# Moving key copies and scalings between VectorE, ScalarE and POOL in the first chunk of a block-sparse attention with an MLP behind it

## The chip, the cores and the metric

The kernel runs on one core of a Trainium2 chip. The metric is the device time of one execution in microseconds (us); lower is better. A core has a matmul engine (TensorE, PE in the profile), VectorE (DVE), ScalarE (ACT), GpSimd (POOL) and a queue that issues DMAs (SyncE, SP). Each engine works through its own queue in order and waits for the others by semaphores.

## The reference

```python
def _attn_ref(q, k, v, sampled_blocks):          # q, k, v: (4, 8, 768, 64)
    scores = scale * np.matmul(q, k.transpose(0, 1, 3, 2))
    # blocks of 32: kept are |i - j| <= 1, the first and last block of
    # rows and of columns, and three sampled blocks per row of blocks
...
    scores = np.where(mask, scores, -1000000000.0)
    attn = np.exp(scores - np.max(scores, axis=-1, keepdims=True))
    attn = attn / (np.sum(attn, axis=-1, keepdims=True) + 1e-09)
    return np.matmul(attn, v)

def _moe_ref(x, w_in, w_out):                    # (3072, 512), (512, 2048), (2048, 512)
    h = np.maximum(x @ w_in, 0.0)
    return h * h @ w_out
```

The attention's output, 3072 tokens of 8 heads x 64, is the input of the second part. The mask is never built: each block of 32 rows gathers eight blocks of keys (first, last, three sampled, three neighbours).

## The kernel before, in words

**Tiles and chunks.** The 3072 tokens are 24 tiles of 128 (four batches of six). The text calls them k0 to k23. A chunk is three tiles. A tile's attention is done in two halves of four heads: k0u0, k0u1, k1u0 and so on (class `Half`, L380). The first and the last block of rows of a batch see all keys; they are done for two heads at a time by class `Whole` (L581), four per batch, W0 to W3 here.

**A half's steps.** `scores` (L427) multiplies queries with gathered keys on TensorE; `maxima` (L444) reduces on VectorE and scales the negative maximum (L453); `exps` (L491) runs four exponentials on ScalarE with that maximum as bias; `turn` (L503) transposes on TensorE; `copies` (L513) takes the transposes out of PSUM on ScalarE; `values` (L524) multiplies with gathered values; `norm` (L540) divides and transposes on VectorE; `high` (L865) casts the result to the matmul's 32-bit format (xh) on POOL, for the very last half on ScalarE; `low` (L869) subtracts it on VectorE to get the rest (xl). `Whole` has the same steps; its `copies` (L676) have two parts (512 and 256 columns), the first on ScalarE, the second on VectorE (L683).

**Keys.** For tiles k0 to k5 the gathered keys (tile `KG`) are copied on chip from a whole batch of keys in SBUF (`kn`). `copy_keys` (L275) is a generator: per half it copies the two static blocks (L338), the neighbouring blocks (L308, or a wide copy of `key_windows`, L303, and two edges, L315), then three sampled blocks for each block of rows (L290), and it yields after each block of rows. Eight such steps make a tile. The generators of k3, k4 and k5 stand in the list `later`, to which `loads` (L553) appends them as the chunk goes on.

**Weights.** A weight block of 128x512 comes by a POOL DMA as 64-bit numbers (`craw`, L785). `cut` (L787) makes 32-bit numbers of it with two ScalarE operations (L801, L803) and `cut_bits` (L806) with two VectorE operations (L812, L813). `cut_next` (L829) issues one round of these stages, each for a different block. `split` (L842) makes a cast (wi, on ScalarE in the first chunk) and a difference (POOL, L848) for the matmuls. Buffers of `craw` and of these split weights rotate through seven.

**The order of work.** Every queue's order is written out by the program. Until the first dense matmul a loop counts steps (`now`, L1044): units W0 to W3, k0u0, ..., k2u1 begin five steps apart, each resumes after the lags of `LAG_0`; at step 8 `prepare` (L1026) issues the rest of the copies for k0 to k2 and five weight loads; from `FIXED_0` on one of the copies in `fixed` (L1038) is issued per step on ScalarE: static values (L212) and the value windows of k2 (L224, L228); at the steps of `CUT_0` a `cut_next`; from step 44 on, at every second step, one step of k3's keys.

**The dense stretch.** Then `moe(0)` (L959) runs the two matmuls of the first chunk: `hidden` (L883) and `project` (L926), 16 blocks each. It yields some six times per block, and at each yield (L1071 to L1081) a step of the first generator in `later` is issued, every third time a `cut_next`, and the second chunk's attention is advanced (halves 12 steps apart from step 0 on, `LAG_1`). Chunks 1 to 7 follow in the same way.

Of the kernel before, what the change touches and what calls it, by code (L numbers as in the profile page):

```python
# [15 lines left out]
ALU = mybir.AluOpType  # L16
# [12 lines left out]
NJ = P // BLK  # L29
# [5 lines left out]
SCALE = 0.125  # L35
# [12 lines left out]
UC = 3  # L48
# [19 lines left out]
G_AT = 6  # L68

STEP_0 = 5  # L70
STEP_1, FIRST_1 = 12, 0
LAG_1 = {**LAG, "v": 10, "x": 3, "t": 6, "v0": 5, "n": 0}
LAG_0 = {"s": 2, "x": 2, "t": 3, "c": 2, "v0": 2, "n": 2, "r": 1, "l": 3, "l0": 8}
SPLIT_0 = 52

CUT_0 = (30, 5)
CUT_1 = 3

KEYS_0, KEYS_1 = 8, 44


FIXED_0 = 7
KEYS_N = 2
MOVED = 6


# [10 lines left out]
def tile_block_sparse_attention_moe(ctx: ExitStack, tc, kd, knd, qd, qgd, vd, vnd, samp, const, wcat, out):  # L97
# [9 lines left out]
    nc = tc.nc  # L107
# [134 lines left out]
    def groups(t):  # L242

        return tuple(range(1 if t == 0 else 0, NJ - 1 if t == NT - 1 else NJ))
# [51 lines left out]
    def key_windows(k, u, copy):  # L296

        b, t = order[k]
        kg, kn = st["kg", b, t][:, :, :, 2 * u : 2 * u + 2], st["kn", b, u]
        if 0 < k < UC:  # L300
            dst = kg[:, :, NJ:NK].rearrange("p j a i c -> p j a (i c)")
            src = kn[:, NJ * t : NJ * t + NJ].rearrange("p a i c -> p a (i c)").unsqueeze(1)
            copy(dst, src.broadcast_to(list(dst.shape)))  # L303
            return
        js = groups(t)
        c = NJ * t + js[0] - 1
        for n in range(3):
            copy(kg[:, js[0] : js[-1] + 1, NJ + place(k, 0, n)], kn[:, c + n : c + n + len(js)])  # L308
# [8 lines left out]
    later = []  # L317
# [62 lines left out]
    class Half:  # L380
# [63 lines left out]
        def maxima(self):  # L444
            m = self.m = rot.tile([P, 2, 2], F32, tag="m", name=f"m{self.name}", bufs=4)
            at = self.rows
            for e in range(2):
                nc.vector.tensor_reduce(  # L448
                    m[at, e], self.sb[e][at].rearrange("p (i c) -> p i c", i=2), axis=AX, op=ALU.max
                )  # L450
            self.p = rot.tile([P, 4, 2, NJ, BLK], F32, tag="p", name=f"p{self.name}", bufs=PBUFS)
            if not self.moved:
                nc.vector.tensor_scalar(m[at], m[at], -SCALE, None, op0=ALU.mult)  # L453
                return
            for e in range(2):
                nc.vector.tensor_tensor(  # L456
                    self.p[at, 2 * e : 2 * e + 2].rearrange("p h c a s -> p h (c a s)"),
                    self.sb[e][at].rearrange("p (i c) -> p i c", i=2),
                    m[at, e].unsqueeze(2).broadcast_to([at.stop, 2, NSLOT]),
                    op=ALU.subtract,  # L460
                )
# [28 lines left out]

        def exps(self):  # L491
            at = self.rows
            for e in range(2):
                for i in range(2):
                    nc.scalar.activation(  # L495
                        self.p[at, 2 * e + i].rearrange("p c a s -> p (c a s)"),
                        self.sb[e][at, i * NSLOT : (i + 1) * NSLOT],
                        AF.Exp,
                        scale=SCALE,
                        bias=self.m[at, e, i : i + 1],  # L500
                    )
# [51 lines left out]
        def loads(self, step):  # L553

            k = order.index((self.b, self.t))
            eng = nc.gpsimd if self.b == 0 else nc.sync
            if step == 0 and self.t == NT - 2 and self.b + 1 < B:
                load_keys(self.b + 1, self.u, eng)
            if step == 0 and self.t == NT - 1 and self.b + 1 < B:
                if self.u == 0:  # L560
                    load_whole(self.b + 1, eng)
                    load_vn(self.b + 1, 0, eng)
            n = k + (UC if k < UC - 1 else UC - 1)
            if step == 0 and self.u == 1 and k != UC - 1 and n < len(order):
                load_q(*order[n])
                if n < 2 * UC:
                    keys_of(*order[n])
                    later.append(copy_keys(*order[n]))
                    next(later[-1])
                elif self.moved:  # L570
                    load_kg(*order[n])
            if step == 1 and self.u == 1 and 2 * UC <= n < len(order):
                load_kg(*order[n])
            n = UC if k == 0 else k + 1
            if step == 2 and k not in range(1, UC) and n < len(order):
                if self.t == NT - 1:
                    load_static(n, self.u)
                load_window(n, self.u)
                load_sampled(n, self.u, nc.sync, SP)

    class Whole:  # L581


        keys = S // 2
# [91 lines left out]
        def copies(self, pt):  # L676
            self.pT = rot.tile([P, S], F32, tag="pT", name=f"pTg{self.name}", bufs=2)
            for i, n in enumerate(self.parts):
                at = i * self.parts[0]
                if i == 0:  # L680
                    nc.scalar.copy(self.pT[:, at : at + n], pt[i][:, :n])
                else:
                    nc.vector.tensor_copy(self.pT[:, at : at + n], pt[i][:, :n])  # L683
# [333 lines left out]
    for k in range(UC):  # L1017
        keys_of(0, k, begin if k == 2 else None)
    for k in range(1, UC):
        key_windows(k, 0, nc.vector.tensor_copy)  # L1020
    first = copy_keys(0, 1)
    deque(copy_keys(0, 0), 0)
    for _ in range(NJ):
        next(first)

    def prepare():  # L1026
        for k in range(1, UC):
            key_windows(k, 1, nc.vector.tensor_copy)
        for _ in range(AHEAD):
            cut_next()  # L1030
        deque(first, 0)
        for f in windows(1, 0) + windows(1, 1):
            f(nc.gpsimd.tensor_copy)
        load_sampled(1, 0, nc.sync, SP, (2,))
        load_sampled(2, 1, nc.sync, SP, (0, 1))
        deque(copy_keys(0, 2), 0)

    fixed = [lambda copy, k=k, i=i: copy_static(k, i, copy) for k in range(UC) for i in range(2)]  # L1038
    fixed += windows(2, 0) + windows(2, 1)
    side = lambda name: ps_o.tile([P, 512], F32, tag="o", name=name)  # L1040
    work = Stream()
    for at, u in units(0):
        work.add(at, 0, lambda u=u: u.run(side, LAG_0))
    now, ahead = 0, None  # L1044
    while work.todo or work.running:
        work.step(now)
        now += 1
        ahead = ahead or (later[0] if later else None)
        if now >= KEYS_1 and now % KEYS_N == 0 and later and later[0] is ahead and next(ahead, True):
            later.pop(0)  # L1050
        if now >= FIXED_0 and fixed:
            fixed.pop(0)(nc.scalar.copy)
            if not fixed:
                load_sampled(2, 1, nc.sync, SP, (2,))
        if now == KEYS_0:
            prepare()
        if now >= CUT_0[0] and (now - CUT_0[0]) % CUT_0[1] == 0:
            cut_next()
        if now == SPLIT_0:
            wi1[0, 1] = split(0, W1[1], "wi0_1")  # L1060
# [7 lines left out]
    now = 0  # L1068
# [71 lines left out]
```

## Time and profile before

| | us |
|---|---|
| median of 3 runs | 744.94 (744.84 to 745.29) |
| the profiled execution's own time | 745.86 |
| its span in the profile | 744.0 |
| TensorE busy | 714.0 (96%) |
| VectorE, ScalarE, POOL busy | 533.0, 500.5, 539.4 |
| DMA moved | 105.22 MB |

Times in the trace count from the start of the span. A busy TensorE is not one at its peak: its matmuls are pipelined, and a matmul's length in the trace is longer than its share of the time. PEclk is the clock that TensorE was granted, 1.00 being full. A wait is put down to what released it last. In a timeline, neighbouring instructions of one line are merged, and "x3" is their number.

### The profile page before, as it was taken

How to read it: one execution, taken by the hardware profiler on the slowest of the kernel's cores; microseconds unless marked ns; L12 is line 12 of the kernel's file. 1: busy time of each engine (PE TensorE's matmuls, PEld its weight loads, DVE VectorE, ACT ScalarE, POOL GpSimd, SP SyncE). 2: the span in 40 equal slices, each digit the busy share in tenths (PEclk: the TensorE clock that was granted, in tenths of full speed). 3: DMA queues.
4: the chain of work that ended last, by engine and by line, in shares of the span. 5: the costliest groups of instructions: out<-in, count | busy, mean ns of one | idle time of the engine just before them, and what ended most of it. 6: DMA issues, size and time to landing. Idle time of an engine off the chain costs nothing.

```text
span 744.0 us, 21519 instructions
## 1 busy us (share of the span) xinstructions
PE 714.0 (96%) x7496; PEld 569.7 (77%) x7496; DVE 533.0 (72%) x1076; ACT 500.5 (67%) x1107; POOL 539.4 (73%) x681
## 2 busy tenths in 40 slices
PE   5869999999999999999999999999999999999997
PEld 2546666567878888877878888877778888888996
DVE  7885766968776877768877786768778686647552
ACT  5875677998875875579776777478866776623222
POOL 7986734249786587769877577877976586868985
PEclk9988999999999999999999999999999999999999
DMA  8785799755555547645455466455355452101001
GB/s 271 226 225 159 206 298 304 179 154 171 146 126 130 174 126 211 145 104 144 104 165 146 100 193 177 132 131 176 95 160 143 100 160 55 34 1 44 1 1 42
DMA packets 94479, 105.22 MB, mean 141 GB/s; under 512 B 13827, under 2 KB 82180, under 8 KB 94372
## 3 DMA queue, kind: packets, MB, share of 16 engines
q1 hardware_dynamic: 88420, 81.00, 41.1%
q0 software_dynamic: 5664, 22.45, 9.2%
q8 instruction: 60, 0.98, 0.6%
q14 instruction: 47, 0.39, 0.2%
q10 hardware_dynamic: 288, 0.39, 0.1%
HBM read 97.50 MB, written 6.29 MB: 140 GB/s over the span
## 4 chain that ended last, share of the span: by engine, by line
PE 72%; DVE 10%; ACT 8%; POOL 5%; issue 3%; DMA 1%; SPq 0%; POOLq 0%; ACTq 0%; DVEq 0%
PE ph L883 30%; PE po L936 26%; PE s L436 5%; PE pv L531 5%; PE po L926 3%; DVE m L448 2%; POOL gl L917 2%; PE pvg L694 2%; POOL pgm L660 1%; ACT craw L803 1%; ACT p L495 1%; POOL wo L848 1%; PE g L624 1%; DVE p L456 1%; DVE pT L487 1%
## 5 line engine op out<-in xcount | busy, mean ns | idle before, releaser
L883 PE MATMUL ph<-xh,wi 128*128 128x384 f32 x960 | 276.1, 348 | 0.6 <-POOL wi L848 0.4
L481 ACT ACTIVATE pm<-p 32x256 f32<-32x256 f32 x528 | 219.3, 415 | 15.4 <-DVE p L456 8.2
L848 POOL TENSOR_TENSOR wi<-W,wi 128x512 fp32r<-128x512 f32 x120 | 163.7, 1364 | 71.8 <-DVE wi L847 36.9
L936 PE MATMUL po<-wo,gh 128*128 128x512 f32 x672 | 211.7, 396 | 0.0
L883 PEld LDWEIGHTS ph<-xh,wi 128*128 128x128 f32 x960 | 173.9, 188 | 23.0 <-issue 10.0
L904 ACT ACTIVATE r<-ph 128x384 f32<-128x384 f32 x128 | 63.0, 492 | 168.2 <-PE ph L883 167.6
L848 POOL TENSOR_TENSOR wo<-WO,wo 128x512 fp32r<-128x512 f32 x112 | 144.9, 1293 | 34.6 <-DVE wo L847 32.9
L917 POOL TENSOR_TENSOR gl<-gf,gh 128x384 fp32r<-128x384 f32 x112 | 119.1, 1063 | 64.1 <-DVE gf L915 54.5
L883 PE MATMUL ph<-xl,wi 128*128 128x384 f32 x480 | 162.4, 338 | 0.0
L936 PEld LDWEIGHTS po<-wo,gh 128*128 128x128 f32 x672 | 123.0, 188 | 27.1 <-issue 7.5
L936 PE MATMUL po<-wo,gl 128*128 128x512 f32 x336 | 134.6, 401 | 5.1 <-POOL gl L917 4.9
L915 DVE SCALAR_TENSOR_TENSOR gf<-ph,r 128x384 f32<-128x384 f32 x112 | 62.0, 553 | 105.7 <-ACT r L904 97.6
L883 PEld LDWEIGHTS ph<-xl,wi 128*128 128x128 f32 x480 | 90.3, 188 | 7.6 <-issue 3.3
L847 DVE CAST wo<-WO 128x512 fp32r<-128x512 f32 x112 | 85.1, 760 | 0.0
L936 PEld LDWEIGHTS po<-wo,gl 128*128 128x128 f32 x336 | 63.0, 187 | 24.6 <-POOL gl L917 11.5
L910 ACT ACTIVATE gh<-r 128x384 fp32r<-128x384 f32 x112 | 59.0, 526 | 10.4 <-ACT r L904 0.4
L448 DVE TENSOR_REDUCE m<-s 128x2 f32<-128x512 f32 (+1 forms) x96 | 61.1, 676 | 3.0 <-PE s L436 3.0
L847 DVE CAST wi<-W 128x512 fp32r<-128x512 f32 x105 | 60.4, 576 | 0.0
L531 PEld LDWEIGHTS pv<-V,pT 128*32 128x32 f32 x2816 | 43.5, 111 | 20.6 <-issue 10.6
L531 PE MATMUL pv<-V,pT 128*32 128x65 f32 x2816 | 52.2, 224 | 5.1 <-DVE xn L548 1.9
L436 PE MATMUL s<-KG,q 64*32 64x256 f32 x1408 | 55.2, 391 | 0.8 <-issue 0.6
L456 DVE TENSOR_TENSOR p<-s,m 128x512 f32<-128x512 f32 (+1 forms) x72 | 45.9, 677 | 0.0
(92 smaller groups left out, 768.1 us busy)
## 6 DMA issues: line engine op xcount, KB each, us to landing
craw<-in_w_dram POOLq DMA_DIRECT2D x32, 512.0 KB, 5.9
V<-in_v_dram SPq DMA_DIRECT2D x462, 32.5 KB, 2.1
KG<-in_k_dram SPq DMA_DIRECT2D x198, 64.0 KB, 1.9
V<-in_v_dram SPq DMA_DIRECT2D x28, 390.0 KB, 5.5
KG<-in_k_dram SPq DMA_DIRECT2D x12, 768.0 KB, 5.9
q<-in_q_dram SPq DMA_DIRECT2D x24, 256.0 KB, 2.8
out_dram<-ot SPq DMA_DIRECT2D x22, 256.0 KB, 5.8
V<-in_v_dram SPq DMA_DIRECT2D x16, 292.5 KB, 6.3
```

Source lines behind the costliest of these rows:

```text
L436: nc.tensor.matmul(self.sb[e][g * BLK : (g + 1) * BLK, i * NSLOT : (i + 1) * NSLOT], q[r, j, pr, :], kg[r, j, :, pr, :], start=True, stop= ...
L448: nc.vector.tensor_reduce(m[at, e], self.sb[e][at].rearrange("p (i c) -> p i c", i=2), axis=AX, op=ALU.max)
L481: nc.scalar.activation(p[a * BLK : (a + 1) * BLK, g], x[g * BLK : (g + 1) * BLK, :, a], AF.Exp, scale=SCALE)
L531: nc.tensor.matmul(po[h * BLK : (h + 1) * BLK, g * VW : (g + 1) * VW], self.pT[:, g, 2 * e + i, c], v[:, self.u, j, h * VW : (h + 1) * VW] ...
L847: nc.vector.tensor_copy(w[:, 0], src)
L848: nc.gpsimd.tensor_tensor(w[:, 1], src, w[:, 0], op=ALU.subtract)
L883: nc.tensor.matmul(ph[c, f][:, :TOK], wi[:, w, cc], x[:, cc], start=(cc == 0 and i == 0), stop=(cc == NCC - 1 and i == 2),)
L904: nc.scalar.activation(r, acc[:, :TOK], AF.Relu)
L910: nc.scalar.activation(gh, r, AF.Square)
L915: nc.vector.scalar_tensor_tensor(gf, acc[:, :TOK], 0.0, r, op0=ALU.max, op1=ALU.mult)
L917: nc.gpsimd.tensor_tensor(gl, gf, gh, op=ALU.subtract)
L936: nc.tensor.matmul(acc[c][u], g[:, at], w[:, k], start=(f == 0 and i == 0), stop=(f == NF - 1 and i == 2))
```

## The change

- The keys of k3 and k4 (tiles four and five) are no longer begun in the first chunk's loop; all steps of `later` are issued in the dense stretch, k5's (tile six) too. `KEYS_1` and `KEYS_N` go, and so does the step that `loads` issued at once.
- The wide key copies of k1 and k2 go from VectorE to ScalarE (first halves of the heads) and to POOL (second halves). On POOL the first half of k1's keys now comes before the second half of k0's.
- The scaling of the negative maximum for k0 to k2 goes from VectorE to ScalarE, into `exps`.
- The second part of the copies of W0 to W3 goes from VectorE to ScalarE.
- The value windows of k2 are split: the second half of the heads goes from ScalarE to POOL, at the end of `prepare`. ScalarE's static copies begin at step 14 instead of 7.
- Weight rounds come at steps 33, 38, 43, 48 and 53 (five) instead of 30, 35, ..., 55 (six).
- The second chunk's halves begin 11 steps apart from step 8 on, instead of 12 apart from step 0 on.

```diff
-STEP_1, FIRST_1 = 12, 0
+STEP_1, FIRST_1 = 11, 8
...
-CUT_0 = (30, 5)
+CUT_0 = range(33, 56, 5)
...
-KEYS_0, KEYS_1 = 8, 44
-FIXED_0 = 7
-KEYS_N = 2
+KEYS_0 = 8
+FIXED_0 = 14
...
             if not self.moved:
-                nc.vector.tensor_scalar(m[at], m[at], -SCALE, None, op0=ALU.mult)
+                if self.k >= UC:
+                    nc.vector.tensor_scalar(m[at], m[at], -SCALE, None, op0=ALU.mult)
                 return
...
         def exps(self):
             at = self.rows
+            if self.k < UC:
+                nc.scalar.mul(self.m[at], self.m[at], -SCALE)
...
                     later.append(copy_keys(*order[n]))
-                    next(later[-1])
...
-                if i == 0:
+                if i == 0 or self.b == 0:
                     nc.scalar.copy(self.pT[:, at : at + n], pt[i][:, :n])
...
-        key_windows(k, 0, nc.vector.tensor_copy)
-    first = copy_keys(0, 1)
-    deque(copy_keys(0, 0), 0)
-    for _ in range(NJ):
-        next(first)
+        key_windows(k, 0, nc.scalar.copy)
+    keys = [copy_keys(0, k) for k in range(UC)]
+    for k in range(2):
+        for _ in groups(k):
+            next(keys[k])
+    deque(keys[0], 0)
 
     def prepare():
-        for k in range(1, UC):
-            key_windows(k, 1, nc.vector.tensor_copy)
         for _ in range(AHEAD):
             cut_next()
-        deque(first, 0)
+        key_windows(1, 1, nc.gpsimd.tensor_copy)
+        deque(keys[1], 0)
         for f in windows(1, 0) + windows(1, 1):
             f(nc.gpsimd.tensor_copy)
         load_sampled(1, 0, nc.sync, SP, (2,))
         load_sampled(2, 1, nc.sync, SP, (0, 1))
-        deque(copy_keys(0, 2), 0)
+        key_windows(2, 1, nc.gpsimd.tensor_copy)
+        deque(keys[2], 0)
+        for f in windows(2, 1):
+            f(nc.gpsimd.tensor_copy)
...
-    fixed += windows(2, 0) + windows(2, 1)
+    fixed += windows(2, 0)
...
-        ahead = ahead or (later[0] if later else None)
-        if now >= KEYS_1 and now % KEYS_N == 0 and later and later[0] is ahead and next(ahead, True):
-            later.pop(0)
...
-        if now >= CUT_0[0] and (now - CUT_0[0]) % CUT_0[1] == 0:
+        if now in CUT_0:
             cut_next()
```

More of the change, by code (lines that the diff above doesn't have):

```diff
@@ L1043, in tile_block_sparse_attention_moe @@
         work.add(at, 0, lambda u=u: u.run(side, LAG_0))
-    now, ahead = 0, None
+    now = 0
     while work.todo or work.running:
```

## The prediction

> **What bounds the kernel now.** I read the page first: the 40 slices (18.6 us each) of TensorE and of its granted clock.
>
> ```profile
> span 744.0 us, 21519 instructions
> ...
> PE   5869999999999999999999999999999999999997
> ...
> PEclk9988999999999999999999999999999999999999
> ```
>
> From the fourth slice on TensorE is full. Only the attention of the first chunk, ahead of the first dense matmul, has holes. So the change is worth the time by which the dense stretch starts earlier, less whatever TensorE loses afterwards. Next, TensorE's timeline (start, length, engine, line, operation; in brackets idle time and its releaser).
>
> ```profile
> 15.39 1.54 PE L673 MATMUL ptg<-ident,pg 128*128 128x128 f32 x6
> ...
> 48.67 1.54 PE L510 MATMUL pt<-ident,p 128*128 128x128 f32 x8 [0.77 <-ACT p L495]
> 52.13 2.31 PE L531 MATMUL pv<-V,pT 128*32 128x65 f32 x64 [1.92 <-DVE xn L548]
> 56.39 0.69 PE L883 MATMUL ph<-xh,WI 128*128 128x384 f32 x1 [1.96 <-POOL xh L867]
> ```
>
> The dense stretch (L883) starts at 56.39, and what ended the wait before it is a POOL cast of k2u0's activations. The windows of 1 us (length; busy time of PE, PEld, DVE, ACT, POOL; then the granted clock) show that it ran at half clock at first:
>
> ```profile
> 60.00:61.00 1.00, 1.00 (x11) 0.92 (x4) 0.75 (x2) 0.00 (x0) 0.00 (x0) 0.50 1.01 227
> 61.00:62.00 1.00, 1.00 (x7) 1.00 (x6) 0.97 (x3) 0.00 (x0) 0.00 (x0) 0.90 0.52 111
> ```
>
> Full clock is back about 61.4, so 5.0 us of dense work ran at half speed: 2.5 us lost. POOL's, SP's and VectorE's timelines before that:
>
> ```profile
> 35.83 1.09 POOL L308 COPY KG<-kn 128x256 f32<-128x256 f32 x3
> ...
> 51.79 0.59 POOL L290 COPY KG<-kn 128x64 f32 x3
> ...
> 54.21 1.25 POOL L848 TENSOR_TENSOR wi<-W,wi 128x512 fp32r<-128x512 f32 x1
> 55.42 0.58 POOL L290 COPY KG<-kn 128x64 f32 x3
> 55.95 0.39 POOL L867 CAST xh<-x 128x256 fp32r<-128x256 f32 x1
> ```
>
> ```profile
> 27.76 15.87 SPq L365 DMA_DIRECT2D V<-in_v_dram  x16
> ```
>
> ```profile
> 41.27 1.52 DVE L453 TENSOR_SCALAR m<-m 128x4 f32<-128x4 f32 x1
> ...
> 47.94 0.17 DVE L453 TENSOR_SCALAR m<-m 128x4 f32<-128x4 f32 x1
> ...
> 52.02 0.45 DVE L376 STREAM_TRANSPOSE x<-xn 128x256 f32<-128x256 f32 x1
> ```
>
> VectorE has k2u0's x ready at 52.47; POOL's cast ends at 56.34, after key copies of tiles k3 and k4 (L290) and a weight subtraction (L848). ScalarE's timeline of the chunk:
>
> ```profile
> 2.04 0.20 ACT L126 ACTIVATE warm<-below 128x1 f32<-128x1 f32 x1
> ...
> 14.53 2.98 ACT L212 COPY V<-V 64x1040 f32<-64x1040 f32 x3
> 17.40 1.07 ACT L224 COPY V<-vn 128x1040 f32<-128x1040 f32 x1
> 18.50 0.40 ACT L228 COPY V<-vn 32x260 f32<-32x260 f32 x1
> 18.93 0.59 ACT L681 COPY pTg<-ptg 128x512 f32<-128x512 f32 x1
> 19.54 1.05 ACT L649 ACTIVATE pg<-g,mb 128x384 f32<-128x384 f32 x2
> ...
> 25.87 1.55 ACT L495 ACTIVATE p<-s,m 96x256 f32<-96x256 f32 x4
> 28.92 0.86 ACT L520 COPY pT<-pt 128x384 f32<-128x384 f32 x2 [1.49 <-PE pt L510]
> ...
> 42.82 1.57 ACT L495 ACTIVATE p<-s,m 128x256 f32<-128x256 f32 x4 [1.49 <-DVE m L453]
> ...
> 48.15 1.58 ACT L495 ACTIVATE p<-s,m 128x256 f32<-128x256 f32 x4 [1.58 <-DVE m L453]
> ...
> 51.32 1.11 ACT L520 COPY pT<-pt 128x512 f32<-128x512 f32 x2
> ```
>
> From 28.92 to 52.43 ScalarE waits only in front of exponentials of k2u0 and k2u1 (1.49 and 1.58 us), both times for VectorE's scaling L453. So three engines share this stage: VectorE holds ScalarE back, ScalarE hands out k2u1's last copies at 52.4, POOL adds the last delay.
>
> **The start of the chunk.** The two 128x1024 key copies of L1021 go from VectorE to ScalarE, which is idle then: about 1.0 us each by the 2.98 us for three of 64x1040. VectorE's first maxima start some 0.5 us earlier. ScalarE gets the second part of all four pTg copies (0.4 us each, an estimate below the 0.59 of the first part, which is twice as wide). The static copies begin at step 14, not 7. That costs something: after W1's exponentials ScalarE has one static copy, then stands idle until W1's transposes (15.39 to 16.9), a stretch that static copies fill now. I replay its queue from W1's first copy at about 16.3: two parts 1.0, W2's exponentials 1.05, five statics 4.8 (23.1), W2's copies 1.0, W3's exponentials 1.0, the three window copies of (2,0) 1.07 and twice 0.4 (27.0), W3's copies 1.0, then the scaling, then k0u0's exponentials 1.55, done at 29.8. Now they are done at 27.4, but TensorE's transposes delay the next copy to 28.92. This part is slower by about 0.9 us.
>
> **The rest of the chunk.** VectorE loses six scalings (0.17 to 1.52 us each), and the bit operations L812/L813 now stand behind the maxima of their round, not ahead of them. From 29.8 each half takes ScalarE about 1.0 for copies, 1.7 for scaling and exponentials and 1.3 for a cut, so it asks for k2u0's maxima at 42.9 and for k2u1's at 46.9. Their scores follow the transposes of k1u0 and k1u1, at 37.5 and 41.5; with 1.3 us of maxima behind at most one other short step they are done near 39.4 and 43.9. Both ScalarE waits go. ScalarE gets five scalings of 128x4 in this stretch. No such ScalarE row exists; the nearest, 128x1, took 0.20 (2.04); the upper bound is the 0.40 of the 32x260 copy; below zero is excluded, since ScalarE is the queue that binds. I take 0.2. Its work from 28.92 to 52.43 is 23.5 - 3.1 = 20.4; with five scalings 21.4; from 29.85 that ends at **51.3**, against 52.43. The weight cuts stay in the same places of ScalarE's queue but the sixth, which moves into the dense stretch. There the steps that need weights call for them: by the sixth step both versions have issued 13 cuts, so "weights come later" costs nothing, covered by the first two matmul blocks.
>
> On POOL the prepared block changes by two 128x1024 key copies (some 1.1 each, an estimate by ScalarE's 1.07 for 1040 columns) and the window copies of (2,1), 1.9; k0's second keys give up their place to k1's first, which fill POOL's wait for the second key load; the weight loads go out some 3 us earlier. I put its end at 36.7, where k3's first keys start at 35.8 now, so k0u0's cast comes no later than now. SP's queue keeps its order: the batch of sampled values for k1 and k2 still waits for POOL's windows of tile 1, at 26.9 by the replay and 27.8 now (L365). Its issue ends at 43.6 now, near 42.7 then; its last rows land about when ScalarE has copied k2u0 (46.9), so a new wait of up to 0.7 us (an estimate) is possible there. It stays in the range.
>
> Then pv of k2u1: 2.31 at half clock (52.13), so 53.6. POOL has no key copies left; its subtraction follows ScalarE's weight cast at 49.1 and ends at 50.4, a load issue follows, and k2u0's cast ends at 51.3, in time. TensorE's dense stretch starts at **53.5**: -2.9. The second halves of k2u1's activations come at about 55.8 (normalizing and transposing some 1.3, the two casts some 0.9), while 12 matmuls of first halves run. What is late next is ScalarE.
>
> **The clock.** Now the hole from 50.2 to 52.13 precedes 10 us at half clock. The new hole, from k2u1's transposes (done 48.9, behind exponentials that end at 48.5) to 51.3, is at least as long, so half clock again is likely. If it ends 5.0 us into the dense stretch as now, nothing is gained (0). If it ends one grid step after 51.2, near 54.6, the dense part loses 0.55 instead of 2.5: -1.95. I take -1.1. The Trainium skill, "TensorE: Matmul & The Clock Gate", section "What's actually happening", lets the clock up after one busy window of about 3.4 us on a free-running grid. That would count pv's 2 us too and favours 54.6, which would make the total 741.8; the trace agrees in so far as the low stretch is 10.2 us long.
>
> **The moved keys.** All of k3's and k4's keys now fall into the dense stretch, and k5's come later in it (steps 20 to 27). The subtraction for W1[6] is queued on POOL behind 63 L290 copies, 18 L308 copies, four more subtractions and nine load issues; TensorE waits for it.
>
> ```profile
> L290 POOL COPY KG<-kn 128x64 f32 x102 | 20.9, 252 | 0.0
> ```
>
> ```profile
> L290 POOL COPY KG<-kn 128x64 f32 x30 | 9.6, 363 | 0.0
> L848 POOL TENSOR_TENSOR wi<-W,wi 128x512 fp32r<-128x512 f32 x4 | 5.1, 1277 | 2.7 <-ACT wi L845 2.7
> L785 POOL DMA_DIRECT2D craw<-in_w_dram x8 | 4.4, 554 | 5.9 <-issue 4.4 <-ACT WO L801 1.4
> ```
>
> ```profile
> 64.24 1.09 POOL L308 COPY KG<-kn 128x256 f32<-128x256 f32 x3
> ...
> 67.05 1.12 POOL L290 COPY KG<-kn 128x64 f32 x6
> ...
> 72.13 1.62 POOL L290 COPY KG<-kn 128x64 f32 x3
> ```
>
> ```profile
> 72.17 0.76 DVE L812 SCALAR_TENSOR_TENSOR W<-W,craw 128x512 int32<-128x512 int32 x1 [2.07 <-ACT craw L803]
> 72.96 0.69 DVE L813 SCALAR_TENSOR_TENSOR W<-craw,W 128x512 int32<-128x512 int32 x1
> ```
>
> ```profile
> 87.92 1.11 PE L531 MATMUL pv<-V,pT 128*32 128x65 f32 x64
> ...
> 92.66 0.74 PE L883 MATMUL ph<-xh,wi 128*128 128x384 f32 x1
> ```
>
> Undisturbed, an L290 copy takes 0.187 (1.12 for six): 63 are 11.8. The L308 copies are 18 x 0.36 = 6.5 (1.09 for three at 64.24), subtractions 5 x 1.28 = 6.4, loads 9 x 0.55 = 5.0: 29.7 us from 51.3 is 81.0, plus about 1.5 while the first load waits for VectorE to free its buffer: 82.5. TensorE needs that weight at 92.66 now, 36.3 us after its start; less 2.5 of half clock and one pv fewer by then (1.1) that is 32.7 of full-speed work, so 53.5 + 0.55 + 32.7 = 86.8. But beside L812/L813 three copies took 1.62, not 0.59: 1.0 more. Eight such pairs fall in this stretch; I count six on POOL copies: 88.5, so TensorE waits **+1.7**. Bounds: 0 without disturbance; 7.3 if every pair blocks POOL for its full 1.45 (82.5 + 11.6 = 94.1). Tile k3's own scores are safe: its first half's keys (3 L308 and 12 L290 copies, 3.3 us, around that first load's wait) are there near 58.3, and the scores come behind 24 dense matmuls (seven in the window from 61 us: some 3.5 us, so 57.5) and two projections.
>
> Sum: -2.9 - 1.1 + 1.7 = -2.3 on the profiled run: span 741.7. The span is 1.86 us short of that run's own time (745.86), which is 0.92 above the median of 744.94; so 743.6 in that run and **742.6** as a median.
>
> **Rivals.** (1) *POOL starves the dense stretch* (slower). Mechanism as above, in place the weights W1[5] to W1[7]: each L812/L813 pair shuts POOL out entirely. For it: L290's mean is 363 ns from 60 to 90 us and 252 before; against it: six copies ran in 1.12 with VectorE busy elsewhere. It decides once TensorE waits over 4.0 us; at 7.3 the time is 744.94 - 4.0 + 7.3 = 748.2. The rule for this is in the Trainium skill, "SBUF — State Buffer", section "Who interferes with whom": a VectorE instruction with two SBUF inputs and a GpSimd one that reads SBUF exclude each other for the whole instruction; the trace agrees in kind, not in full (three copies took 1.62, not 0.59, so 1.0 was lost beside a pair of 1.45). (2) *ScalarE eats the gain*: the late static copies and the scalings, at 0.4 instead of 0.2, keep its last copies at 52.4, so only POOL's wait goes (about 1.8 us) and the moved keys cost as much: 744.9, no change. For it: ScalarE then stands idle ahead of W1's copies, where static copies keep it busy now. Against it: 3.1 us of its waits for VectorE go. (3) *All goes well*: clock up by 54.6 and POOL in time: -2.9 - 1.95 = 740.1, and 739 if pv runs at full clock too.
>
> **How the numbers follow.** About 0.2% (1.5 us) is what a measurement of this kernel can tell from no change. Forecast 0.40 (its own range 741.2 to 743.4); rival 3 0.20; rival 2 0.25; rival 1 0.15. Faster takes the forecast and rival 3: 0.60; same is rival 2: 0.25; slower rival 1: 0.15. The range leaves out a tenth on each side: 739.4 up to 746.8, half-way into rival 1.
>
> **What would show it.** Right: the first L883 near 53.5 (this shows the seam's sum), ScalarE with no waits between k0u1's exponentials and k2u1's copies, k0u0's exponentials ending 2 us later than now, no L453 in the first chunk, L290 absent before the first L883 but for tiles k0 to k2, short waits of ph for POOL's wi before 95 us. Wrong: waits for POOL's wi above 4 us in sum, ScalarE's last copies at 52 or later, or waits of ScalarE for VectorE's maxima that stay.

## The result and the profile after

The kernel after takes **751.87 us** (median of 6 runs, 749.01 to 754.76); the kernel before 745.16 beside it (744.84 to 746.11). The ratio is 1.0086, 95% interval 1.0060 to 1.0112: slower by 6.7 us, where 2.3 us faster was forecast, and outside the range. The profiled run took 751.54, its span 749.8 (744.0 before).

The page of the kernel after, and TensorE's timeline at the places that matter (start, length, engine, line, operation; in brackets idle time and its releaser; lines are shifted by one or two against the kernel before):

```profile
span 749.8 us, 21511 instructions
...
PE   5779899799999999999999999999999999999997
...
PEclk9899999899999999999999999999999999999999
```

```profile
53.42 0.69 PE L884 MATMUL ph<-xh,WI 128*128 128x384 f32 x1
...
80.83 1.96 PE L533 MATMUL pv<-V,pT 128*32 128x65 f32 x64 [3.37 <-ACT pT L522]
...
135.09 2.17 PE L435 MATMUL s<-KG,q 64*32 64x256 f32 x24 [5.58 <-DMA V<-in_v_dram]
```

The dense stretch starts at 53.42, with no wait, as forecast (53.5). But two waits follow that the kernel before does not have: 3.37 us at the values of tile k3's first half (L533) and 5.58 us at the scores of tile k6's first half (L435). The granted clock falls to half (0.50) during each. These are the windows of both kernels, before first (length; busy time of PE, PEld, DVE, ACT, POOL; granted clock, DMA share, GB/s):

```profile
56.00:80.00 24.00, 23.48 (x203) 15.77 (x204) 12.97 (x24) 13.82 (x27) 16.44 (x43) 0.89 0.62 183
80.00:100.00 20.00, 19.69 (x198) 12.62 (x197) 13.29 (x25) 14.43 (x29) 12.05 (x28) 1.00 0.80 234
...
120.00:140.00 20.00, 19.04 (x168) 11.95 (x168) 15.05 (x25) 16.16 (x33) 7.38 (x10) 1.00 0.99 289
```

```profile
56.00:80.00 24.00, 21.20 (x144) 14.26 (x142) 17.26 (x23) 15.27 (x29) 21.09 (x54) 0.99 0.55 170
80.00:100.00 20.00, 19.17 (x220) 13.22 (x221) 13.16 (x22) 14.45 (x30) 15.70 (x38) 0.91 0.77 248
...
120.00:140.00 20.00, 14.42 (x138) 9.04 (x138) 11.71 (x21) 13.27 (x27) 6.59 (x9) 0.83 0.87 266
```

From 56 to 80 us the clock is better than before (0.99 against 0.89), from 80 to 100 and from 120 to 140 it is worse. How far the kernel is ahead is read from the ReLUs of the first chunk's dense part on ScalarE: the first, the twelfth and (already the second chunk's first) the seventeenth, before and after.

```profile
63.39 0.49 ACT L904 ACTIVATE r<-ph 128x384 f32<-128x384 f32 x1 [3.59 <-PE ph L883]
...
134.87 0.50 ACT L904 ACTIVATE r<-ph 128x384 f32<-128x384 f32 x1
...
165.71 0.49 ACT L904 ACTIVATE r<-ph 128x384 f32<-128x384 f32 x1
```

```profile
58.36 0.49 ACT L905 ACTIVATE r<-ph 128x384 f32<-128x384 f32 x1 [1.83 <-PE ph L884]
...
131.02 0.49 ACT L905 ACTIVATE r<-ph 128x384 f32<-128x384 f32 x1
...
170.53 0.49 ACT L905 ACTIVATE r<-ph 128x384 f32<-128x384 f32 x1
```

At the first ReLU the change is 5.0 us ahead, at the twelfth 3.9 (the attention steps between them stand at other places, so single lags swing by a few us), at the seventeenth 4.8 behind. So the seam, as the text calls the place where the first chunk's attention ends and the dense stretch starts, brought the profiled run 5 us, and the dense stretch with the second chunk's attention in it lost twice as much.

The next rows show what each wait stood behind. ScalarE, VectorE and POOL ahead of the first, SP's queue ahead of the second (the issue, and in the row behind it KB and median us from issue to landing); last the same issue and the same scores in the kernel before:

```profile
79.68 0.62 ACT L846 CAST wi<-W 128x512 fp32r<-128x512 f32 x1 [5.04 <-DVE WO L814]
80.20 0.58 ACT L522 COPY pT<-pt 128x512 f32<-128x512 f32 x1
```

```profile
72.56 0.78 DVE L813 SCALAR_TENSOR_TENSOR W<-W,craw 128x512 int32<-128x512 int32 x1 [2.09 <-ACT craw L804]
73.37 2.58 DVE L814 SCALAR_TENSOR_TENSOR W<-craw,W 128x512 int32<-128x512 int32 x1
75.87 0.68 DVE L524 COPY pT<-pt 128x512 f32<-128x512 f32 x1
76.47 1.27 DVE L447 TENSOR_REDUCE m<-s 128x2 f32<-128x512 f32 x2
...
78.06 0.81 DVE L813 SCALAR_TENSOR_TENSOR WO<-WO,craw 128x512 int32<-128x512 int32 x1
78.90 0.69 DVE L814 SCALAR_TENSOR_TENSOR WO<-craw,WO 128x512 int32<-128x512 int32 x1
```

```profile
73.56 0.53 POOL L786 DMA_DIRECT2D craw<-in_w_dram  x1
74.11 1.28 POOL L849 TENSOR_TENSOR wi<-W,wi 128x512 fp32r<-128x512 f32 x1
```

```profile
124.28 0.48 SPq L331 DMA_DIRECT2D KG<-in_k_dram  x1
```

```profile
KG<-in_k_dram SPq DMA_DIRECT2D x1, 576.0 KB, 10.6
```

```profile
121.07 0.40 SPq L332 DMA_DIRECT2D KG<-in_k_dram  x1
```

```profile
131.68 0.59 PE L436 MATMUL s<-KG,q 64*32 64x256 f32 x2 [0.64 <-issue]
```

ScalarE's copy of k3u0's probabilities (80.20, L522) is queued behind the cast of W1[5], block 5 of the first matmul's weights (79.68, L846), which had stood 5.04 us. That cast needs a buffer of the ring of seven that holds both raw weights and casts; the buffer comes free with the bits of a piece of WO (78.90 plus 0.69). Those stand on VectorE behind a copy, k3u1's maxima and the bits of W1[5], whose second instruction took 2.58 instead of 0.69 while POOL issued a weight load (73.56) and made a subtraction (74.11). That excess, 1.9 us, is a part of the cast's 5.04. The second wait is plainer: the last load of k6's keys (576 KB) is issued at 124.28, 3.2 us later than before, lands 10.6 us later (10.5 before), and TensorE is at that place 1.5 us earlier than before. (The bracket at 135.09 names a load of V, the next on the same queue; that it is the keys is shown by the times here and by a_kg6 below.)

### The profile page after: what moved, and what is told of

It is laid out like the page before. It is cut to its first block, busy times and chain, and to the rows that moved or that the text cites. A ratio compares the mean times of both kernels' runs of the same rounds, so it can differ in the third digit from the quotient of the medians.

```text
span 749.8 us, 21511 instructions
## 1 busy us (share of the span) xinstructions
PE 712.6 (95%) x7496; PEld 571.2 (76%) x7496; DVE 533.1 (71%) x1062; ACT 503.0 (67%) x1116; POOL 539.7 (72%) x686
## 4 chain that ended last, share of the span: by engine, by line
PE 70%; DVE 9%; ACT 7%; POOL 5%; DMA 5%; issue 2%; SPq 1%; ACTq 0%; POOLq 0%; DVEq 0%
PE ph L884 29%; PE po L937 26%; PE s L435 5%; PE pv L533 5%; DMA V<-in_v_dram 3%; PE po L927 2%; PE pvg L695 2%; POOL gl L918 2%; PE g L625 2%; POOL pgm L661 1%; DVE m L447 1%; ACT craw L804 1%; ACT p L497 1%; POOL wo L849 1%; DMA KG<-in_k_dram 1%
## 5 line engine op out<-in xcount | busy, mean ns | idle before, releaser
L533 PEld LDWEIGHTS pv<-V,pT 128*32 128x32 f32 x2816 | 43.6, 111 | 26.1 <-ACT pT L522 12.1
L533 PE MATMUL pv<-V,pT 128*32 128x65 f32 x2816 | 52.5, 224 | 8.4 <-ACT pT L522 8.2
L435 PE MATMUL s<-KG,q 64*32 64x256 f32 x1408 | 54.6, 390 | 5.6 <-DMA V<-in_v_dram 5.6
L927 PE MATMUL po<-WO,gp 128*128 128x512 f32 x96 | 46.9, 615 | 0.1
```

The source lines that it names most:

```text
L435: nc.tensor.matmul(self.sb[e][g * BLK : (g + 1) * BLK, i * NSLOT : (i + 1) * NSLOT], q[r, j, pr, :], kg[r, j, :, pr, :], start=True, stop= ...
L533: nc.tensor.matmul(po[h * BLK : (h + 1) * BLK, g * VW : (g + 1) * VW], self.pT[:, g, 2 * e + i, c], v[:, self.u, j, h * VW : (h + 1) * VW] ...
L927: nc.tensor.matmul(acc[c][u], g[:, u * P : (u + 1) * P], WO[f], start=(f == 0), stop=(f == NF - 1))
```

## The experiments

Every ratio is to runs of the kernel before on the same chip, with its 95% interval; a smaller one is faster.

**First: which part makes which wait.** e1_step is the kernel before with the second chunk's new steps alone; e2_exps spreads the second chunk's exponentials otherwise; e3_no4 leaves the copies of tile k4's sampled keys out (its scores there lack those keys); e4_holes gives k3's keys back to the first chunk and takes the old steps.

```diff
e1_step (before)   +STEP_1, FIRST_1 = 11, 8
e2_exps (after)    -LAG_1: "x": 3, "t": 6     +LAG_1: "x": 1, "t": 8
e3_no4 (after)     +for r in range(0 if k == 4 else NRAND):
e4_holes (after)   +STEP_1, FIRST_1 = 12, 0
                   +KEYS_3 = (35, 36, 37, 40, 41, 42, 45, 46, 47)
                   ... (used as in m_holes below)
```

> The kernel before with one edit, the second chunk's halves 11 steps apart from step 8 on. Theory A (two stalls: the first comes from POOL's moved key copies that hold VectorE's L814 and, through ScalarE's weight cast, k3u0's values; the second from the new steps alone, which put k5u1's exponentials and k6u0's scores into one step, so that the scores wait for a PSUM bank): the second stall appears near 130 us and the first does not; 749 to 752 us. Theory B1 (the first stall comes from the new steps too, because k3u0's copies now stand behind a weight cast in ScalarE's queue): both stalls, 753 to 757. If neither stall comes from the steps: 744 to 746.

> The changed kernel with the second chunk's exponentials two steps earlier (lag x 1 instead of 3, t 8 instead of 6; nothing else moves). Theory A: the wait of 5.6 us of k6u0's scores shrinks below 1.5 us, and the low clock behind it goes: 744 to 747 us. Theory B2 (the scores wait for k6's DMAs, as the profile puts it): wait and time unchanged, 750 to 753.

> The changed kernel without the sampled key copies of tile k4 (24 POOL copies are left out, so those keys are stale). Theory A: POOL is done with keys some 5 us earlier, L814 is no longer held for 2.6 us, the wait of k3u0's values (3.4 us) falls below 1 us, the second stall stays: 746 to 748.5 us. Theory B1: the wait of k3u0's values stays at 3 us or more, 750 to 753.

> The changed kernel with k3's keys in POOL's idle time of the first chunk (steps 35 to 47, after the scalings and copies have left VectorE) and the second chunk at 12 steps from step 0, as in the kernel before. Theory A: the dense stretch starts at 53.4 to 54.5 and neither stall is there: 740 to 742.5 us. Rival: the copies hold VectorE's bit operations and the casts in the first chunk, the dense stretch starts after 55: 743 to 746 us.

Measured: e1_step 750.67, ratio 1.0044 [1.0026, 1.0062]; e2_exps 753.07, 1.0096 [1.0079, 1.0113]; e3_no4 751.27, 1.0062 [1.0037, 1.0087]; e4_holes 744.88, 0.9986 [0.9976, 0.9995]. In e1_step, whose first chunk is that of before, TensorE's second wait is there and the first nearly gone. (Its profiled run is the longest of its seven, 753.06.) The last row is its load of k6's keys:

```profile
80.45 1.14 PE L531 MATMUL pv<-V,pT 128*32 128x65 f32 x64 [0.61 <-ACT pT L520]
...
136.46 2.20 PE L436 MATMUL s<-KG,q 64*32 64x256 f32 x24 [7.05 <-DMA KG<-in_k_dram]
```

```profile
126.98 0.40 SPq L332 DMA_DIRECT2D KG<-in_k_dram  x1
```

So the new steps make the second wait without any moved key: the load goes out 5.9 us later than in the kernel before (121.07), and TensorE wants it 1.6 us earlier (129.41 against 131.04), although the dense stretch starts at 56.05, hardly earlier than before. It stays in e2_exps (5.2 us), so that the banks that exponentials hold are not its cause, and the theory of them fell. It shrinks, to 3.0, in e3_no4, where the first one stays at 2.92: k4's keys cause little of that one, and theory A's "below 1 us" and its time were wrong. With k3's keys back in the first chunk and the old steps (e4_holes) there is no wait at k3's values, one of 0.80 at k6's scores and one of 1.56 for a weight part of POOL's at 87.11. The dense stretch starts at 54.77, and the kernel is slightly faster than before; the time is the rival's, 2.4 us above theory A's.

**Second: k6's keys, the ring, the weights' rounds.** a_kg6 asks for k6's keys right behind k4u1's scores instead of behind its copies. a_ahead4 loads weights four rounds ahead, which frees the ring's buffers a round earlier. a_both4 does both. a_cut has the weight rounds of before.

```diff
a_kg6      -elif self.moved:             +elif self.moved or n == 2 * UC:   (step 0)
           -2 * UC <= n < len(order)     +2 * UC < n < len(order)           (step 1)
a_ahead4   -AHEAD = 5                    +AHEAD = 4
a_both4    both of these
a_cut      -CUT_0 = range(33, 56, 5)     +CUT_0 = range(30, 70, 5)
```

> The kernel after, but the keys of tile 6 are asked for right after tile 4's second scores and not 11 of TensorE's yields later, behind that half's copies. Theory (the transfer of tile 6's keys, issued at 124.28 in the trace of after and 10.6 us in landing, holds TensorE for 5.58 us and costs 1.8 more by the half clock behind it): the transfer starts some 8 us earlier, the wait at tile 6's first scores is under 1 us, and the time is 744.5 to 747. What could be late next: the queue's load of V's window and q, which it is moved ahead of. Rival (TensorE has no work of its own left there, so that another wait stands in its place): 750 to 753, with a wait of 4 us or more on another row between 120 and 140.

> The kernel after, with the weights' loads four rounds ahead of their cutting in place of five, the cutting itself at the same steps. Theory: the cast of W1's block 5 on ScalarE (79.68, 5.04 us idle) waits through the seven rotating buffers for the piece of WO whose bits VectorE makes last (78.06 to 79.59), and the copy of tile 3's probabilities stands behind that cast. One round less in flight frees a buffer a round earlier: the cast starts by 77, TensorE's wait at tile 3's values (3.37) is under 0.7, the half clock behind it goes, and the time is 746 to 749 (the wait for tile 6's keys stays, 5 to 6). Rival (the cast waits for its own block's bits, which POOL's key copies hold up, or for the weight's transfer): wait and time as after, 750 to 754, or slower if the loads now land late.

> The kernel after with both edits: tile 6's keys asked for earlier, and the weights' loads four rounds ahead in place of five. Theory: both waits gone, 739.5 to 743, that is the gain at the seam (about 3 at the start of the dense stretch) and nothing given back. Rival (the gain at the seam is given back in any case, because the weights' chain paces the first dense stretch): 744 to 747, the same as before.

> The kernel after, with the weights' rounds of the first chunk again from step 30 on, every 5 steps, as in the kernel before. Theory (ring and steps, not the later weights): the wait at tile 3's values shrinks by at most half, since the chain starts a round or two ahead but still stands behind the same ring; tile 6's keys wait as in after; 748 to 752. Rival (the later weights are what costs): both the cast's wait and TensorE's 3.37 go, 745.5 to 748.

a_kg6 took 746.52, ratio 1.0022 [1.0010, 1.0033], inside the theory's times; in the kernel after the ratio was 1.0086. Its SP queue and TensorE:

```profile
116.60 0.40 SPq L331 DMA_DIRECT2D KG<-in_k_dram  x1
```

```profile
81.44 1.96 PE L533 MATMUL pv<-V,pT 128*32 128x65 f32 x64 [4.30 <-ACT pT L522]
...
131.50 1.29 PE L435 MATMUL s<-KG,q 64*32 64x256 f32 x22 [1.14 <-DMA V<-in_v_dram]
```

The load goes out 7.7 us earlier, the wait at k6's scores is 1.14 instead of 5.58 (m_step_kg6 below has 1.13 in the same place, put down to ScalarE's copies, so that the keys need not be its cause), and 0.64% of the time is gone, some 4.8 us (between two sets of runs). By the ratios the same edit takes 5.6 us from a_ahead4 (a_both4) and 2.9 from e1_step (m_step_kg6). That settles the second wait. The first stays, 4.30 here.

The other three show what that one is made of. a_ahead4 took 753.22, 1.0121 [1.0094, 1.0148]; a_cut 754.56, 1.0130 [1.0112, 1.0148]; a_both4 749.38, 1.0046 [1.0030, 1.0062]. The first two are no faster than after (1.0060 to 1.0112). In a_ahead4 the cast of W1[5] is no longer held, and TensorE waits for something else:

```profile
72.26 0.60 ACT L846 CAST wi<-W 128x512 fp32r<-128x512 f32 x1
72.77 0.58 ACT L522 COPY pT<-pt 128x512 f32<-128x512 f32 x1
```

```profile
75.30 0.62 PE L884 MATMUL ph<-xh,wi 128*128 128x384 f32 x2 [1.08 <-POOL wi L849]
...
83.81 0.62 PE L884 MATMUL ph<-xh,wi 128*128 128x384 f32 x2 [2.33 <-POOL wi L849]
...
91.55 0.61 PE L884 MATMUL ph<-xh,wi 128*128 128x384 f32 x2 [0.69 <-POOL wi L849]
...
136.40 2.17 PE L435 MATMUL s<-KG,q 64*32 64x256 f32 x24 [8.81 <-DMA V<-in_v_dram]
```

The cast comes at 72.26 without a wait, which fits the ring as what held it; the wait at k3's values goes. In its place stand three waits for POOL's part of wi, 4.1 us in sum, and k6's keys are later still (8.81). In a_cut, where the chain of casts starts earlier, the same three places wait 1.22, 1.06 and 1.67. The theory's time was 4.2 us too low for a_ahead4 (753.22 lies in the rival's range, with other waits than the rival's) and 2.6 too low for a_cut; a_both4 lies 2.4 us above even the rival's range. It waits 3.3 us for POOL's part of wi, and also 3.00 us for V's sampled rows at 136.98, which now stand behind k6's keys in SP's queue; in the first chunk it waits 0.44, 1.89 and 1.87 us for other sampled rows of V.

**Third: POOL.** All four have k6's keys asked for early. m_step_kg6 is e1_step with that. m_cut_no4 is a_cut with it and without the copies of k4's sampled keys (left out of its scores). m_holes makes five of the eight pieces of k3's keys in the first chunk again (the expectations count nine: the ninth call copies nothing and only takes the finished tile off the list), where POOL idles; m_holes_cut has the weight rounds of before too.

```diff
m_holes      +KEYS_3 = (36, 41, 42, 46, 47)
             +if now in KEYS_3 and later and next(later[0], True):
             +    later.pop(0)
```

> The kernel before with the second chunk's new steps (11 apart, from 8 on), and tile 6's keys asked for right after tile 4's second scores. Theory (by themselves the new steps cost only through the transfer of tile 6's keys): the wait of 7.05 at tile 6's first scores goes and the time is that of before, 744.5 to 747. Rival (the new steps bunch the second chunk's work against the weights' transfers): 748 to 751.

> The kernel after with tile 6's keys asked for earlier, the first chunk's weight rounds again from step 30 on, and without the 24 copies of tile 4's sampled keys, which leaves those keys out of the scores. Theory F (two queues stand one behind the other: with the chain of casts a round ahead, TensorE waits for POOL's parts of wi instead, 3.9 in all, because the moved keys fill POOL): without tile 4's copies those waits are under 1.0, the wait at tile 3's values is under 1, tile 6's under 1.5, and the time is 740 to 743.5. Rival G (transfers or the chain of casts hold TensorE in any case): waits of 3 or more between 56 and 100, 746 or more.

> The kernel after with tile 6's keys asked for earlier, and with five of the nine pieces of tile 3's keys made on POOL in the first chunk again, at steps 36, 41, 42, 46 and 47, where POOL's queue idles in the trace of after. Theory F: POOL is some 7 us freer in the first dense stretch, but the cast of W1's block 5 still waits through the ring, so that TensorE's wait at tile 3's values stays at 2 to 4: 743 to 747. Rival (POOL's keys alone cause the wait): it is under 1, 740 to 743.

> The same, with the first chunk's weight rounds from step 30 on as well. Theory F (both queues relieved): waits for POOL's wi under 1.5 in all, at tile 3's values under 1, the dense stretch begins by 54; 740 to 743.5, under both kernels. Rival G: as long as with the five pieces alone, or the first chunk's end is held up by the added work on POOL (dense stretch from 55 on): 744 to 748.

Measured: m_step_kg6 746.36, 1.0005 [0.9990, 1.0019]: with k6's keys early the new steps cost nothing that shows, as the theory had it. m_cut_no4 743.46, 0.9975 [0.9961, 0.9989]: the waits for wi are gone, one of 2.24 at k3's values is left, where I expected under 1; the time is just inside theory F's. **m_holes 744.00, 0.9979 [0.9966, 0.9992]**, a little faster than the kernel before, at theory F's time but with under 1 us at k3's values, the rival's mark. m_holes_cut 744.34, 0.9987 [0.9973, 1.0001], is no better: its waits are those of theory F (1.09 for wi, 0.53 at k3's values, the dense stretch from 52.33), and another of 0.96 at 88.18, but the time is the rival's. TensorE, VectorE and POOL of m_holes, the latter two at the place of the row of 2.58:

```profile
53.03 0.44 PE L885 MATMUL ph<-xh,WI 128*128 128x384 f32 x1
...
75.59 0.62 PE L885 MATMUL ph<-xh,wi 128*128 128x384 f32 x2 [1.81 <-POOL wi L850]
...
78.14 1.14 PE L534 MATMUL pv<-V,pT 128*32 128x65 f32 x64 [0.54 <-ACT pT L523]
```

```profile
71.55 0.70 DVE L814 SCALAR_TENSOR_TENSOR W<-W,craw 128x512 int32<-128x512 int32 x1 [2.10 <-ACT craw L805]
72.28 0.69 DVE L815 SCALAR_TENSOR_TENSOR W<-craw,W 128x512 int32<-128x512 int32 x1
```

```profile
73.72 0.53 POOL L787 DMA_DIRECT2D craw<-in_w_dram  x1
74.27 1.27 POOL L850 TENSOR_TENSOR wi<-W,wi 128x512 fp32r<-128x512 f32 x1
```

VectorE's pair (0.70 and 0.69) is done before POOL's load issue and subtraction begin. TensorE's waits ahead of k3's values come to 1.81 and 0.54, against 4.30 in a_kg6, and no clock dip follows (the windows from 56 to 140 us all read 1.00).

**Fourth: the copy's place, or the keys.** n_first (a_kg6 with the second chunk's turns, which are TensorE's transposes, and copies three yields earlier) puts the copy ahead of the cast; n_first_holes has the five pieces as well; n_allkeys has all of k3's keys in the first chunk and the lags of after.

```diff
n_first      -LAG_1: "t": 6, "v0": 5     +LAG_1: "t": 3, "v0": 8
n_allkeys    +KEYS_3 = (35, 36, 37, 40, 41, 42, 45, 46, 47)
```

> The kernel after with tile 6's keys asked for earlier, and with the second chunk's turns and copies three of TensorE's yields earlier, the values where they were, so that ScalarE's copy of tile 3's probabilities stands ahead of the cast of W1's block 5. Theory C (the copy's place behind that cast makes the wait): the wait at tile 3's values, 4.30 with the keys alone, is under 0.5; TensorE then runs on to the next thing that is late, POOL's part of wi, 1 to 2.5 in all; 743.5 to 745.5. Rival H (the chain of casts itself holds TensorE, wherever the copy stands): waits for wi of 3 or more between 56 and 100, and 746 to 748, as with the keys alone.

> The same, with five of the nine pieces of tile 3's keys made in the first chunk again (steps 36, 41, 42, 46 and 47). Theory C: no wait over 1 between 53 and 125 but one for POOL's wi of at most 2; 741.5 to 743.5. Rival H: 743.5 to 745, as with the five pieces and the old place of the copy.

> The kernel after with tile 6's keys asked for earlier and all nine pieces of tile 3's keys made in the first chunk again (steps 35 to 37, 40 to 42, 45 to 47). Theory F (moved keys on POOL cost both the waits for wi and some 2 us of VectorE's bits): no wait for POOL's wi, at tile 3's values under 0.7, but the first chunk ends 0.5 to 1.5 later on POOL; 743 to 745. Rival (the steps and the ring, not the keys): a wait of 2 to 4 at tile 3's values as in after; 745.5 to 747.5.

n_first took 747.93, 1.0036 [1.0024, 1.0047]; n_first_holes 745.02, 0.9995 [0.9983, 1.0007]; n_allkeys 744.41, 0.9990 [0.9977, 1.0003]. In n_first there is no wait at k3's values, as expected, but TensorE's turns now come too early for the exponentials:

```profile
69.50 1.53 PE L512 MATMUL pt<-ident,p 128*128 128x128 f32 x8 [1.62 <-ACT p L497]
...
97.33 1.63 PE L512 MATMUL pt<-ident,p 128*128 128x128 f32 x8 [1.99 <-ACT p L497]
```

That moves the wait and gains nothing: the time is rival H's. n_first_holes waits 1.50 and 1.68 us at the same two turns, so that these waits come from the new lags more than from the keys; its time is above theory C's range. With all of k3's keys back (n_allkeys) no wait for wi is left, one of 1.87 at k3's values is (under 0.7 was expected), and the time is that of m_holes within the intervals.

Taken together: after 1.0086; with k6's keys early 1.0022; with k3's keys back as well 0.9979 to 0.9990. While POOL makes all the moved keys, TensorE loses 3.3 to 4.6 us between 56 and 100 us wherever the queues are cut: at k3's values (after 3.37, a_kg6 4.30) or for wi (a_both4 3.3; a_ahead4 4.1; a_cut 3.95, and 0.61 at k3's values). With k3's keys back and the lags of after it is 1.87 (n_allkeys), 2.35 (m_holes) and 2.6 (m_holes_cut). With only k4's sampled copies left out it is 2.92 (e3_no4) or 2.24 (m_cut_no4). What is left with k3's keys back was not taken apart further.

## Why the prediction was wrong

**The seam came out right in the profiled run, in part by luck.** The dense stretch starts at 53.42 (53.5 forecast). k0u0's exponentials end at 29.85 (29.8), and ScalarE's scalings took 0.21 to 0.25 each (0.2). But its last copies end 0.9 later than forecast, at 52.23 (51.3), since the replay left out that the first of them waits 0.99 us for TensorE's transposes:

```profile
30.84 0.86 ACT L522 COPY pT<-pt 128x384 f32<-128x384 f32 x2 [0.99 <-PE pt L512]
...
51.15 1.08 ACT L522 COPY pT<-pt 128x512 f32<-128x512 f32 x2
```

```profile
52.28 1.21 PE L533 MATMUL pv<-V,pT 128*32 128x65 f32 x62 [0.18 <-ACT pT L522]
```

The values of k2u1 made up for it: they ran at full clock, and their last 62 matmuls took 1.21 us, where I had counted 2.31 for all 64 at half clock.

Nor does every run start there. The first chunk of e2_exps, e3_no4, a_kg6 and n_first is that of the kernel after, and their dense stretches start at 52.51, 55.13, 54.49 and 54.42 (the kernel before, e1_step and m_step_kg6 share the old first chunk: 56.39, 56.05 and 56.33). In the three late ones TensorE waits for V's sampled rows, 2.93, 3.36 and 4.07 us in sum; the kernel after has no such wait and e2_exps 0.18. I had seen this wait coming, sized it at "up to 0.7 us" and left it out of the sum. In a_kg6:

```profile
49.38 1.39 PE L533 MATMUL pv<-V,pT 128*32 128x65 f32 x40 [3.36 <-DMA V<-in_v_dram]
...
54.49 0.45 PE L884 MATMUL ph<-xh,WI 128*128 128x384 f32 x1
```

**The clock** was right in kind: full speed is back at about 56.6 (the window from 56 to 58 us has 0.86), so that 3.2 us of dense work run at half clock, 1.6 lost instead of 2.5: a gain of 0.9 where I took 1.1. The 54.6 that I drew from the Trainium skill ("TensorE: Matmul & The Clock Gate", "What's actually happening") came 2 us later: the low stretch has the length that I gave it, 3.4 us, but it begins at 53.1 and not at 51.2.

**The moved keys: the wait was named wrongly and the term sized too small.** I put it at +1.7, as TensorE's waits for POOL's parts of W1[5] to W1[7]. In the kernel after there is no such wait; the cost shows at k3's values, 3.37 us and some 1.5 lost to half clock behind it (TensorE works at 0.50 from 80.8 to 83.9). POOL was later than I had it, done with W1[6]'s subtraction at 91.0 and not at 88.5, but TensorE, held up at k3's values, did not get there earlier. I followed POOL's queue to its own user, TensorE, and counted only how VectorE holds POOL. But the row of 2.58 shows VectorE's bits held beside POOL as well, and through the ring these held ScalarE. That row explains 1.9 us of the wait at most: in n_allkeys, where the same pair takes 1.00 and 0.69, TensorE still waits 1.87 at k3's values. Giving k3's keys back is worth 2.4 us (n_allkeys, from 1.0022 to 0.9990) to 3.2 (m_holes, 0.9979), inside the bound of 7.3.

**The step that failed is the sum**, "-2.9 - 1.1 + 1.7". It has no term for the second chunk's new steps (11 apart, from 8 on), although I set the change's worth at the earlier start "less whatever TensorE loses afterwards". I followed SP's queue to 43.6 us, where "SP's queue keeps its order", and stopped. The steps set when k6's keys are asked for and how much of the second chunk's work stands ahead of k6's scores: asked for 3.2 us later, wanted 1.5 us earlier (135.09 - 5.58 = 129.51, against 131.68 - 0.64 = 131.04 before). That costs 5.58 us in the profiled run, and some 1.7 by the half clock behind it, and 4.8 us by a_kg6. e1_step has it without the rest of the change, with nearly the old start, so that it is the steps and not the earlier start that make it.

By the ratios the sum is: k6's keys +4.8, k3's keys +2.4 to +3.2, and what is left of the gain at the seam -0.7 to -1.6 (n_allkeys, m_holes; e4_holes, with the old steps, -1.0), where -4.0 was forecast for start and clock together. They add up to the 0.86% found because each is a difference of ratios, and each is uncertain by 1 to 2 us; n_allkeys' interval reaches past 1. The -0.7 to -1.6 still holds the waits of 1.87 and 2.35 us that n_allkeys and m_holes have left, and the runs with late rows of V. The rival "POOL starves the dense stretch" had the right sign and the nearest time (748.2), by a part of the cause and so by luck; waits for wi of over 4 us in sum, which I named as its mark, appear only in a_ahead4, where the ring is relieved. "Weights come later costs nothing" held: with the old rounds, m_holes_cut is no faster than m_holes, and a_cut no faster than after.

**What stays open.** In the profiled runs of m_holes and n_allkeys the dense stretch starts at 53.03 and 52.29, 3.4 and 4.1 us ahead of before, and the spans are 2.7 and 3.0 shorter; by the ratios only 0.7 to 1.6 us are left. In part that is the choice of run: these two took 743.11 and 742.81, 0.9 and 1.6 below their medians, and the profiled run of before 745.86, 0.7 above its own. Their times scatter over 3 to 5 us, those of the kernel before in the same sets of runs over 3 to 4. In the profiled run of m_cut_no4, the longest of its ten (746.97 at a median of 743.46), the first chunk waits 4.04 us for V's sampled rows at 53.03, and the dense stretch starts at 57.30. That late rows of V take the gain from some of the runs is likely, but was not tried by itself.

## What to carry to other kernels

An earlier start is worth only what the next stretch can take: before counting it, follow every queue that the change re-times (here SP's key loads 70 us later) up to the first use of what it brings. And one profiled run is not the start: five runs of one and the same first chunk reached the dense stretch between 52.5 and 55.1. When an engine between two others is filled up, the wait shows wherever the first in-order queue is crossed, so cutting one crossing only moves it; take the load away instead. A step number in a hand-written schedule is a set of transfers with due times, and has to be priced as one.

## What the hardware showed

- VectorE is held beside POOL, not only the reverse: a bit operation of VectorE that overlaps a POOL subtraction of 128x512 took 2.58 and 2.39 us (after, 73.37 and 89.17), 2.45 (a_kg6) and 3.00 (n_first), against 0.69 in m_holes, where it ended before the subtraction began. The Trainium skill, "SBUF — State Buffer", section "Who interferes with whom", makes the shared port an exclusive lock between the two engines, and so in both directions; these rows agree in that VectorE can be the one that is held. They don't show which had the port first: all four begin 0.5 to 0.7 us ahead of the subtraction, about when POOL issues a weight load, and end 0.6 to 1.0 us after it. I had used the rule in one direction.
- How long TensorE waits does not alone decide on half clock: 3.37 us brought it (after, 80.5 to 83.9), 2.33 in a_ahead4 did not (1.00 from 78 to 92), and 1.68 in n_first_holes did (94.7 to 98.2). Once it came, it lasted 3.4 us in both, and twice or three times that elsewhere: 6.8 (after, 131.7 to 138.5) and 10.2 (before, 51.0 to 61.2).
- The same load of 576 KB landed 10.6 us after its issue at 124.28 and 5.9 us after an issue at 116.60 (a_kg6).
